# A fused attention and expert kernel: another order of the first loads, constants and attention steps, with added idle products

## The chip, the cores and the metric

The kernel runs on one core of a Trainium2 chip. The metric is the device time of one execution in microseconds; of several executions the median stands.

## The reference

Attention has two parts: a coarse one on means of four positions, and a local one in which each position sees those less than four away. Their sum, with the heads joined, is the input of a layer of eight experts, of which each row takes the one with the largest router value.

```python
q_d = q.reshape(B, H, Sd, 4, D).mean(axis=3)          # k_d, v_d likewise
out_up = np.repeat(sm_attn(q_d, k_d, v_d), 4, axis=2)
mask = np.abs(pos[:, None] - pos[None, :]) < 4
out_local = np.matmul(softmax(np.where(mask, scale * q @ k.T, -1e9)), v)
x = (out_up + out_local).transpose(0, 2, 1, 3).reshape(B * S, H * D)    # 4608 x 512
logits = x @ w_gate + modality_bias[modality_id]
e_idx = np.argmax(logits, axis=1)
for e in range(8):
    rows = e_idx == e
    out[rows] = gate_w[rows, None] * (np.maximum(x[rows] @ w1[e], 0.0) @ w2[e])
```

q, k and v are (8, 8, 576, 64) in f32; w1 is (8, 512, 1024) and w2 (8, 1024, 512).

## The kernel before, in words

Attention is cut into 32 steps n: batch n // 4, two heads in each. q and k come in halves of a batch, that is for two steps at a time (half h serves steps 2h and 2h + 1), into four pairs of buffers that take turns (called xh, xl, w and xh again in the trace); v comes by batch, in pieces of 90 KB for batch 0 and of 180 KB afterwards, into two windows (h_167, h_168). A step is a chain over all engines. PE transposes q and k (tp, L352) and their fourth rows (tpt, L365), ScalarE and DVE copy them out and sum them (qT, kT, kd L408); PE writes the band mask (mk, L417) and adds the local scores on it (sc, L426), and makes the coarse scores (scd, L449); DVE and ScalarE make the softmax (lm, le, exp, dm, de, z, zr); PE transposes the coarse weights (pdt, L513) and multiplies with v (avd L528, avl L544); DVE adds both into X (L552).

After a batch the router works on it: products with wg (lg, L612), the largest value, a count of rows for each expert, a scatter of row numbers into the table tab (L727, GpSimd), and a store of the rows to xs (L721, SyncE). For these it needs small constants: numbers 0 to 7 and a triangle of ones (`Consts.routing`), w_gate (`Consts.load`), the modalities and their biases (`Consts.biases`), and blank rows in xs and tab (`Router.start`).

Then come the experts, in units of rows. A unit's w1 is loaded raw by SyncE (L945; w2 at L947) into a ring of four buffers, and each piece is split into a high and a low part (hi by GpSimd or ScalarE at L959, lo by DVE or GpSimd at L965), since a product in this precision is made of three: hi with xh, hi with xl, lo with xh. Layer 1 of the first unit (L1136) begins while the last attention steps run: eight groups of twelve products, each group in one bank of PSUM, taken out by ScalarE (relu, L1140) and DVE (what the relu left, L1142). Layer 2 is at L1296. The units behind it use w1 in combined quarters (L1013 for the differences R, L989 and L990 for their split).

The order of the work in attention is written out by hand. Each piece of a step is a call with a key (such as `tpt:4`) and a time, which is n plus `PHASE` plus an offset from `MOVED`; all calls are sorted by that time and issued under a manual schedule, so that this order is each engine's order:

```python
def call(key, at, f, *args):
    at += MOVED.get(key, 0)
    calls.append((at, len(calls), f, args))
```

The loads of q and k (`q0` ...), v (`v00` ...), the constants (`consts`, `routing`, `start`, `biases`) and the first expert's weights and products are calls in the same list. Behind it the routing of the last batch and everything of the experts is put in order by the framework, by its own estimate of when operands are ready, after what the list issued. Idle products (L1464, eight in a group, 128x128 on zeros, into a corner of the bank Z that nobody reads) stand at two places late in the list.

The profile's names are those of the program: xh, xl and w are reused for other things; h_167 and h_168 are the two windows of v; raw is a raw weight piece.

Of the kernel before, what the change touches and what calls it, by code (L numbers as in the profile page):

```python
# [10 lines left out]
I32 = mybir.dt.int32  # L11
# [114 lines left out]
LOP = (0, 3, 4)  # L126
NL = 1
CHP = (4,)
NDA = (2, 4, 8, 10)
ZD = (1, 5, 7, 8, 9, 10)  # L130
XA = (0, 1, 2, 3)
FZ = (21, 23)
FN = 8
NZ = 24


def whole(pieces):

# [1494 lines left out]
```

## Time and profile before

| | |
|---|---|
| median of 3 executions | 652.12 us (649.57 to 653.86) |
| the profiled execution | 645.31 us, of which the span of its trace is 643.6 us |
| mean granted clock of TensorE in it | 0.988 |
| busy: PE, DVE, ACT, GpSimd (POOL) | 615.6, 488.9, 392.2, 300.8 us |

The profile comes from one execution. PE is TensorE's products, DVE is VectorE, ACT is ScalarE, POOL is GpSimd, and SP is SyncE, which issues most transfers. "Idle before" is the time an engine stood still ahead of an instruction, with what released it. The granted clock is 1.00 at 2.4 GHz and 0.50 at 1.2 GHz.

### The profile page before, as it was taken

The numbers are of one execution on the slowest core, as the hardware profiler recorded it, in microseconds if no ns is written. First come the engines' busy times: TensorE is split into PE (matmuls) and PEld (weight loads), VectorE is DVE, ScalarE is ACT, GpSimd is POOL, SyncE is SP. The second block draws the span as 40 slices with busy tenths as digits, with TensorE's granted clock in tenths as the row PEclk, the third lists the DMA queues.
The fourth block names the chain that finished last, engine by engine and source line by source line (L and its number), as shares of the span: only waits on it lengthen the run. The fifth ranks groups of instructions, "written<-read, shape, count | busy, mean of one in ns | idle before, by whom it ended". The sixth has DMA issues, their size and how long they took to land.

```text
span 643.6 us, 19370 instructions
## 1 busy us (share of the span) xinstructions
PE 615.6 (96%) x7414; PEld 516.9 (80%) x7414; DVE 488.9 (76%) x1025; ACT 392.2 (61%) x853; POOL 300.8 (47%) x356
## 2 busy tenths in 40 slices
PE   7699999999999899999999999999999999999995
PEld 4467777776766668889898898998988989989984
DVE  5667888989879858778869889788596886845450
ACT  5568878777877723466564655665665665645451
POOL 7657889889778793570410402304215023030111
PEclk9889999999999899999999999999999999999999
DMA  9799999999979866295553552635633525576821
GB/s 184 155 187 193 184 200 200 191 190 210 184 165 212 227 174 172 60 326 141 165 184 118 166 156 100 195 100 167 193 118 131 148 98 164 135 230 188 223 90 39
DMA packets 173121, 107.16 MB, mean 166 GB/s; under 512 B 132988, under 2 KB 151456, under 8 KB 173026
## 3 DMA queue, kind: packets, MB, share of 16 engines
q1 hardware_dynamic: 165810, 86.71, 56.8%
q0 software_dynamic: 7216, 19.18, 9.3%
q8 instruction: 60, 0.98, 0.7%
q14 instruction: 35, 0.29, 0.2%
HBM read 86.61 MB, written 19.51 MB: 165 GB/s over the span
## 4 chain that ended last, share of the span: by engine, by line
PE 73%; DVE 8%; DMA 6%; SPq 4%; POOL 4%; issue 3%; ACT 1%; POOLq 0%; DVEq 0%; ACTq 0%
PE l L1296 27%; PE l L1197 20%; PE l L1171 3%; DMA raw<-in_moe_w_dram 3%; PE tp L352 3%; PE scd L449 3%; PE avl L544 2%; PE sc L426 2%; PE avd L528 2%; PE xt L1088 2%; SPq L308 2%; SPq L328 1%; PE vp L340 1%; PE pdt L513 1%; PE l L1136 1%
## 5 line engine op out<-in xcount | busy, mean ns | idle before, releaser
L1307 POOL DMA_INDIRECT out_dram<-o,tg x33 | 43.7, 1326 | 165.1 <-ACT o L1299 75.9
L1296 PE MATMUL l<-whi,h 128*128 128x512 f32 (+1 forms) x356 | 109.6, 389 | 0.2 <-DVE h L1274 0.2
L1296 PEld LDWEIGHTS l<-whi,h 128*128 128x128 f32 x356 | 65.2, 188 | 13.1 <-DVE h L1274 0.5
L965 DVE TENSOR_TENSOR wlo<-raw,whi 128x1024 fp32r<-128x1024 f32 x36 | 43.7, 1230 | 33.5 <-ACT whi L959 33.0
L1296 PE MATMUL l<-wlo,h 128*128 128x512 f32 (+1 forms) x178 | 67.9, 385 | 0.0
L1197 PE MATMUL l<-xh,whi 128*128 128x256 f32 x240 | 66.3, 276 | 0.0
L1197 PE MATMUL l<-xl,whi 128*128 128x256 f32 x240 | 66.3, 276 | 0.0
L1197 PE MATMUL l<-xh,wlo 128*128 128x256 f32 x240 | 66.3, 276 | 0.0
L1296 PE MATMUL l<-whl,h 128*128 128x512 f32 (+1 forms) x240 | 57.9, 386 | 0.0
L1212 ACT ACTIVATE h<-R 128x512 fp32r<-128x512 f32 x42 | 26.4, 634 | 41.8 <-DVE R L1210 41.8
L1296 PEld LDWEIGHTS l<-whl,h 128*128 128x128 f32 x240 | 44.0, 188 | 8.6
L1057 POOL DMA_INDIRECT xg<-xs,tg x32 | 39.1, 1221 | 24.3 <-PE xt L1088 16.1
L727 POOL DMA_INDIRECT tab<-ig,si x36 | 36.5, 1014 | 21.5 <-DVE si L698 13.9
L1197 PEld LDWEIGHTS l<-xh,whi 128*128 128x128 f32 x240 | 45.1, 188 | 0.0
L1197 PEld LDWEIGHTS l<-xl,whi 128*128 128x128 f32 x240 | 45.1, 188 | 0.0
L1197 PEld LDWEIGHTS l<-xh,wlo 128*128 128x128 f32 x240 | 45.0, 188 | 0.0
L383 ACT COPY kT<-tp 64x512 f32<-64x512 f32 x64 | 37.3, 582 | 7.8 <-PE tp L352 7.1
L1197 PE MATMUL l<-xh,w 128*128 128x256 f32 x176 | 41.7, 276 | 0.0
L503 POOL TENSOR_TENSOR h<-lt,sel 128x576 f32<-128x576 f32 x32 | 36.8, 1150 | 4.8 <-DVE lt L498 2.8
L1296 PEld LDWEIGHTS l<-wlo,h 128*128 128x128 f32 x178 | 33.2, 188 | 6.7
L959 ACT CAST whi<-raw 128x1024 fp32r<-128x1024 f32 x32 | 33.1, 1049 | 8.3 <-issue 5.0
L1299 ACT ACTIVATE o<-l,tg 128x512 f32<-128x512 f32 x37 | 25.4, 686 | 20.4 <-PE l L1296 16.9
(336 smaller groups left out, 1775.1 us busy)
## 6 DMA issues: line engine op xcount, KB each, us to landing
raw<-in_moe_w_dram SPq DMA_DIRECT2D x176, 128.0 KB
raw<-in_moe_w_dram SPq DMA_DIRECT2D x44, 512.0 KB
h<-in_v_dram SPq DMA_DIRECT2D x53, 180.0 KB
xs<-R SPq DMA_DIRECT2D x64, 128.0 KB
xl<-in_k_dram SPq DMA_DIRECT2D x16, 288.0 KB
xh<-in_q_dram SPq DMA_DIRECT2D x14, 288.0 KB
xl<-in_q_dram SPq DMA_DIRECT2D x8, 288.0 KB
w<-in_k_dram SPq DMA_DIRECT2D x8, 288.0 KB
```

The source lines that it names most:

```text
L352: s.nc.tensor.transpose(p[:, 128 * j : 128 * j + 128], src[:, 5 * (n % 2) + j].rearrange("p a d -> p (a d)"), s.C.ident)
L383: s.nc.scalar.copy(s.kB[r, g, a, PAD + 64 * g : PAD + 64 * g + 512], s.t["tp", "k", n][r])
L503: s.nc.gpsimd.tensor_tensor(s.Pw[n % NPW], s.t.pop(("lt", n))[:, :, :SUB].unsqueeze(2).broadcast_to(sh), s.C.sel.unsqueeze(1).unsqueeze(3) ...
L727: i = nc.gpsimd.indirect_dma_start(out=s.tab[:, :], out_offset=bass.IndirectOffsetOnAxis(ap=C.si[:, t : t + 1], axis=0), in_=C.ig[:, t, :] ...
L959: (nc.gpsimd.tensor_copy if turn in HIP else nc.scalar.copy)(hi, raw)
L965: (nc.gpsimd if turn in LOP else nc.vector).tensor_tensor(lo, raw, hi.bitcast(F32), op=ALU.subtract)
L1057: nc.gpsimd.indirect_dma_start(out=R[:, h, :], out_offset=None, in_=s.xs[:n, :], in_offset=bass.IndirectOffsetOnAxis(ap=T[:, h, 0:1], axis ...
L1197: nc.tensor.matmul(banks[g][:, f, :], a[:, fs], b[:, x, k, :], start=start and f == k == i == 0, stop=k == 1 and i == 2, skip_group_check= ...
L1212: nc.scalar.activation(h, x, AF.Relu)
L1296: nc.tensor.matmul(p[:, cs], a[:, f, hs], x[:, f % 2, cs], start=(f == 0 and i == 0), stop=(f == 7 and i == 2), skip_group_check=last_rows)
L1299: nc.scalar.mul(o, p, T[:, h, 1:2].bitcast(F32))
L1307: nc.gpsimd.indirect_dma_start(out=s.out[:, :], out_offset=bass.IndirectOffsetOnAxis(ap=T[:, h, 0:1], axis=0), in_=o, in_offset=None, boun ...
```

## The change

Calls are cut smaller and get new times. q and k of a half are loaded by calls of their own (`k2`, `q2`, ...; half 0 in four parts, q ahead of k). `Consts.load` loses the modalities and biases to `load_bias`; the DVE part of `routing` becomes `numbers`; `Router.start` is split into `scratch` (the bank Z, first of all), `start`, and `blanks`. `warm` adds groups of `FM` = 6 idle products at five of twelve places, `y0`, `y3`, `y4`, `y8` and `y10`. About 300 keys of steps 0 to 10 get offsets in `MOVED`, or other ones. Nothing that is computed changes. Lines of the changed kernel are 48 to 59 higher (tp L406, tpt L419, sc L480, layer 1 L1195, its evictions L1199 and L1201, R L1072).

```diff
 MOVED = {
...
+    "blanks": 5.8766, ... "k2": -0.4342, "k3": -3.5596, "k4": 1.3137, ... "mi": 6.7344, "numbers": 3.5421,
+    "q2": -0.2781, "q3": -3.6701, "q4": -0.8408, ... "start": 3.1539, "tpt:4": -0.124, ... "wg": 7.5204,
...
+FY = (0, 3, 4, 8, 10)
+FM = 6
...
-    def load(s, tc, pool, work, rows, mid, bias, w_gate):
+    def load(s, tc, pool, w_gate):
...
+    def load_bias(s, tc, work, rows, mid, bias):
+        nc = tc.nc
         s.mf = rows.tile([128, 2 * DM], F32, name="R", bufs=NR)[:36, :384]
...
+    def numbers(s, tc, pool):
+        nc = tc.nc
         s.ef = pool.tile([128, NE], F32, name="ef")
-        nc.vector.tensor_copy(s.ef, ie)
+        nc.vector.tensor_copy(s.ef, s.ie)
...
-    def load_qk(s, b, half):
+    def load_qk(s, h, x, part=None):
         nc = s.nc
-        qt, kt = s.QKt[(2 * b + half) % 4]
-        for j in (slice(0, 5), slice(5, 9)) if (b, half) == (0, 0) else (slice(0, 9),):
-            for t, src in ((kt, s.k), (qt, s.q)):
-                for a in range(2):
-                    h = src[b, 4 * half + 2 * a : 4 * half + 2 * a + 2].rearrange("h s d -> (h s) d")
-                    nc.sync.dma_start(t[:, j, a], h.rearrange("(j p) d -> p j d", p=128)[:, j])
-        s.QK[2 * b + half] = (qt, kt)
+        b, half = divmod(h, 2)
+        s.QK[h] = s.QKt[h % 4]
+        src, j = (s.q, s.k)[x], slice(0, 9) if part is None else (slice(0, 5), slice(5, 9))[part]
+        for a in range(2):
+            g = src[b, 4 * half + 2 * a : 4 * half + 2 * a + 2].rearrange("h s d -> (h s) d")
+            nc.sync.dma_start(s.QK[h][x][:, j, a], g.rearrange("(j p) d -> p j d", p=128)[:, j])
...
-    def start(s, work):
-        nc, xs, tab = s.nc, s.xs, s.tab
+    def scratch(s):
         s.Z = s.ps.tile([128, 512], F32, name="Z", tag="Z", bufs=1)
+
+    def start(s):
+        nc = s.nc
         s.rev = s.Z[:, 0:NE]
...
+    def blanks(s, work):
+        nc, xs, tab = s.nc, s.xs, s.tab
         zr = work.tile([128, DM // 128], F32, name="zr")
...
-            for j in range(3):
-                call(f"q{j}", -3 + 0.1 * (j if j < 2 else 6), at.load_qk, j // 2, j % 2)
+            for j in range(4):
+                call(f"k0{j}", -3 + 0.01 * j, at.load_qk, 0, 1 - j % 2, j // 2)
+            for j in (1, 2):
+                for x, nm in ((1, "k"), (0, "q")):
+                    call(f"{nm}{j}", -3 + 0.1 * (j if j < 2 else 6) - 0.001 * x, at.load_qk, j, x)
+            call("scratch", -3.2, ro.scratch)
...
+            def warm(k):
+                if k in FY:
+                    for _ in range(FM):
+                        nc.tensor.matmul(ro.Z[:, 384:512], C.dummy, C.dummy, start=True, stop=True, skip_group_check=True)
+
+            for k in range(12):
+                call(f"y{k}", 0.7 + 0.7 * k, warm, k)
```

What the change moves on an engine is seen in the engines' orders. On SyncE, at the start of the program, from the last load of half 1 on (half 2 is xl<-in_k and xh<-in_q below the v, in_v), there stood before:

```order
L308 DMA xl<-in_q_dram 128x9x64 x2
L322 DMA h_167<-in_v_dram 27x64
L328 DMA h_167<-in_v_dram 30x11x64
L328 DMA h_167<-in_v_dram 30x12x64 x15
L308 DMA xl<-in_k_dram 128x9x64 x2
L308 DMA xh<-in_q_dram 128x9x64 x2
L206 DMA wg<-in_moe_w_gate_dram 64x2x8 x4
```

and there stand now:

```order
L363 DMA xl<-in_q_dram 128x9x64 x2
L376 DMA h_167<-in_v_dram 27x64
L382 DMA h_167<-in_v_dram 30x11x64
L382 DMA h_167<-in_v_dram 30x12x64 x7
L363 DMA xl<-in_k_dram 128x9x64 x2
L363 DMA xh<-in_q_dram 128x9x64 x2
L382 DMA h_167<-in_v_dram 30x12x64 x8
L363 DMA w_165<-in_q_dram 128x9x64 x2
L363 DMA w_166<-in_k_dram 128x9x64 x2
```

Eight pieces of v have gone behind half 2; half 3 (w_165, w_166) has come right behind them, and wg stands far below.

On PE, around the first products of half 2 (xl is its k, xh its q), where the transposes of step 4 and the scores of step 3 stand, the order before was

```order
L417 LDWEIGHTS identb
L417 MATMUL sc<-mask,identb 128x384
L352 MATMUL tp<-ident,xl 128x128 x4
L426 MATMUL sc<-kT,qT 24x64 x24
L365 MATMUL tpt<-ident,xh 128x128
L365 MATMUL tpt<-ident,xl 128x128
L449 MATMUL scd<-kd_176,h_167 64x144 x6
```

and is now

```order
L471 LDWEIGHTS identb
L471 MATMUL sc<-mask,identb 128x384
L419 MATMUL tpt<-ident,xh 128x128
L419 MATMUL tpt<-ident,xl 128x128
L480 MATMUL sc<-kT,qT 24x64 x24
L406 MATMUL tp<-ident,xl 128x128 x4
L503 MATMUL scd<-kd_176,h_167 64x144 x6
```

The two rows of tpt, which need q of half 2, have gone ahead of the scores (L426, now L480) and of the transposes of k (L352, now L406).

On DVE, where layer 1 of the first unit is taken out of PSUM (h is the eviction, l a bank of layer 1, wlo a low weight part, R the differences of the second unit's raw weights), the order before was

```order
L965 TENSOR_TENSOR wlo_5428<-raw,whi_5427 128x1024 [waits Pool_49]
L965 TENSOR_TENSOR wlo_5446<-raw,whi_5445 128x1024 [waits DMAHW1_49,Activation_49]
L1142 SCALAR_TENSOR_TENSOR h_5304<-l_5483,h_5304 128x512 [waits Activation_49]
L965 TENSOR_TENSOR wlo_5434<-raw,whi_5433 128x1024 [waits Pool_49]
L965 TENSOR_TENSOR wlo_5440<-raw,whi_5439 128x1024 [waits DMAHW4_49,Pool_49]
L742 COPY mc<-cp 128x8 [waits PE_49]
L1013 TENSOR_TENSOR R<-raw 128x512 [waits DMAHW3_49,DMAHW6_49,DMAHW2_49,DMAHW7_49,DMAHW1_49,DMAHW0_49]
L691 TENSOR_TENSOR sl<-pr,oh 128x40 [waits PE_49]
L1142 SCALAR_TENSOR_TENSOR h_5305<-l_5569,h_5305 128x512 [waits Activation_49]
L990 TENSOR_TENSOR whl<-raw,whl 128x512 [waits Activation_49]
```

with the evictions of three other groups above it, and is now (from the last wlo of this unit on)

```order
L1024 TENSOR_TENSOR wlo_5476<-raw,whi_5475 128x1024 [waits DMAHW5_49,Activation_49]
L1072 TENSOR_TENSOR R<-raw 128x512 [waits DMAHW6_49,DMAHW7_49,DMAHW1_49,DMAHW0_49]
L832 SCALAR_TENSOR_TENSOR poff<-pexcl,pbase 128x8 [waits DVE_49]
L844 TENSOR_TENSOR o<-pexcl,uf 128x48 [waits DMAHW4_49,DMAHW3_49,DMAHW2_49]
L1049 TENSOR_TENSOR whl<-raw,whl 128x512 [waits Activation_49]
L846 TENSOR_TENSOR o<-o 128x48 [waits DVE_49]
L1201 SCALAR_TENSOR_TENSOR h_5334<-l_5336,h_5334 128x512 [waits Activation_49]
L1072 TENSOR_TENSOR R<-raw,R 128x512 [waits DMAHW4_49,DMAHW5_49,DMAHW3_49,DMAHW2_49]
L850 TENSOR_TENSOR o<-o,poff 128x48 [waits DVE_49]
L1201 SCALAR_TENSOR_TENSOR h_5334<-l_5513,h_5334 128x512 [waits Activation_49]
L1072 TENSOR_TENSOR R<-raw 128x512
```

All eight evictions of layer 1 (L1142, now L1201) stand behind the first R<-raw now; before, four of them stood ahead of it. The waits in brackets name counters: DMAHW are transfers.

## Rows read from the trace of the kernel before

**Rows 1.** Page, part 1: busy time, share of the span, instructions of each engine.

```profile
PE 615.6 (96%) x7414; PEld 516.9 (80%) x7414; DVE 488.9 (76%) x1025; ACT 392.2 (61%) x853; POOL 300.8 (47%) x356
```

**Rows 2.** Windows: stretch, length, busy us of each engine, PEclk, DMA share, GB/s.

```profile
160.00:200.00 40.00, 38.51 (x918) 28.41 (x922) 33.25 (x103) 31.98 (x103) 31.57 (x41) 1.00 0.92 178
...
240.00:600.00 360.00, 359.00 (x2314) 323.88 (x2314) 281.88 (x449) 207.27 (x306) 98.34 (x84) 1.00 0.53 159
```

**Rows 3.** Windows of the start and of one later stretch.

```profile
8.00:16.00 8.00, 5.65 (x128) 4.32 (x128) 3.83 (x9) 6.02 (x15) 5.22 (x23) 1.00 1.14 195
...
27.26:37.50 10.24, 9.40 (x142) 7.32 (x145) 3.83 (x10) 5.04 (x16) 5.60 (x7) 0.50 0.83 137
...
221.80:225.30 3.50, 3.34 (x57) 2.97 (x49) 3.01 (x12) 2.04 (x8) 2.48 (x3) 0.51 0.72 263
```

**Rows 4.** Waits of PE, 0 to 50 us: total us, times, longest us.

```profile
PE sc L417 <- DVE e L237: 1.8, 1, 1.8
...
PE tpt L365 <- DMA xl<-in_q_dram: 0.8, 1, 0.8
```

**Rows 5.** Timeline of PE: start us, us, instruction xcount [idle before <-releaser].

```profile
18.12 0.87 PE L426 MATMUL sc<-kT,qT 128*24 128x64 f32 x48
...
22.87 0.34 PE L417 MATMUL sc<-mask,identb 128*128 128x384 bf16 x1
24.96 0.63 PE L352 MATMUL tp<-ident,xl 128*128 128x128 f32 x4 [1.75 <-DMA xl<-in_k_dram]
...
28.10 0.45 PE L365 MATMUL tpt<-ident,xh 128*128 128x128 f32 x1 [1.71 <-DMA xh<-in_q_dram]
...
36.09 1.50 PE L426 MATMUL sc<-kT,qT 128*24 128x64 f32 x48
...
43.80 0.66 PE L352 MATMUL tp<-ident,w 128*128 128x128 f32 x4 [1.06 <-DVE kd L408]
```

**Rows 6.** Chain of waits in order of time: start us, us, what.

```profile
22.12 5.89 DMA xh<-in_q_dram
28.10 0.66 PE tpt L365 x2
...
195.68 7.42 DMA h<-in_v_dram
203.12 5.11 DMA raw<-in_moe_w_dram
```

**Rows 7.** DMA view, 0 to 50 us: rate in 40 slices, issues with sizes.

```profile
GB/s 0 76 227 261 225 224 219 221 218 228 193 116 185 196 194 153 169 251 242 224 197 26 9 33 84 239 176 196 199 185 208 221 182 158 145 211 168 190 190 175
...
h<-in_v_dram SPq DMA_DIRECT2D x15, 90.0 KB
```

**Rows 8.** Timeline of PE around the idle products, 216 to 218 us.

```profile
216.84 0.62 PE L1464 MATMUL Z<-dummy 128*128 128x128 bf16 x8
```

**Rows 9.** Instructions of L727, 0 to 120 us: ns min/median/max, first and last start.

```profile
L727 POOL DMA_INDIRECT tab<-ig,si x10: 1010/1010/1194, 70.0 to 119.8; - x10
```

**Rows 10.** Timelines of DVE and ACT, 247 to 253 us.

```profile
247.10 0.68 DVE L1142 SCALAR_TENSOR_TENSOR h<-l,h 128x512 fp32r<-128x512 f32 x1
...
252.53 0.69 DVE L1013 TENSOR_TENSOR R<-raw 128x512 f32<-128x512 f32 x1 [2.40 <-DMA raw<-in_moe_w_dram]
...
252.51 0.62 ACT L989 CAST whl<-raw 128x512 fp32r<-128x512 f32 x1 [2.25 <-DMA raw<-in_moe_w_dram]
```

**Rows 11.** Timeline of GpSimd, 233 to 239 us.

```profile
233.49 2.40 POOL L965 TENSOR_TENSOR w<-raw,w 128x1024 fp32r<-128x1024 f32 x1
...
238.84 3.02 POOL L959 CAST whi<-raw 128x1024 fp32r<-128x1024 f32 x3
```

**Rows 12.** Timeline of PE in layer 1 and at layer 2's start.

```profile
244.64 0.39 PE L1136 MATMUL l<-xh,whi 128*128 128x512 f32 x1
...
246.91 0.39 PE L1136 MATMUL l<-xh,whi 128*128 128x512 f32 x1
...
255.85 0.61 PE L1296 MATMUL l<-whi,h 128*128 128x512 f32 x2
```

More of the change, by code (lines that the diff above doesn't have):

```diff
@@ L212, in load, with routing @@
         nc.sync.dma_start(s.bb, bias.unsqueeze(0).broadcast_to([128, 2, NE]))
-    def routing(s, tc, pool, work, psum):
+    def routing(s, tc, pool, work):
         nc = tc.nc
@@ L225, in routing @@
         s.si = pool.tile([128, 36], I32, name="si")
-        ie = work.tile([128, NE], I32, name="ie")
-        nc.gpsimd.iota(ie, pattern=[[1, NE]], base=0, channel_multiplier=0)
+        s.ie = work.tile([128, NE], I32, name="ie")
+        nc.gpsimd.iota(s.ie, pattern=[[1, NE]], base=0, channel_multiplier=0)
+        s.iu = work.tile([128, NUMAX], I32, name="iu")
+        nc.gpsimd.iota(s.iu, pattern=[[1, NUMAX]], base=0, channel_multiplier=0)
+    def numbers(s, tc, pool):
+        nc = tc.nc
         s.ef = pool.tile([128, NE], F32, name="ef")
-        nc.vector.tensor_copy(s.ef, ie)
+        nc.vector.tensor_copy(s.ef, s.ie)
         s.rev = pool.tile([128, NE], F32, name="rev")
@@ L238, in routing @@
         s.e2 = s.e2.rearrange("p t e -> p (t e)")
-        iu = work.tile([128, NUMAX], I32, name="iu")
-        nc.gpsimd.iota(iu, pattern=[[1, NUMAX]], base=0, channel_multiplier=0)
         s.uf = pool.tile([128, NUMAX], F32, name="uf")
-        nc.vector.tensor_copy(s.uf, iu)
+        nc.vector.tensor_copy(s.uf, s.iu)
         n = 2 * NE
@@ L1356, in call @@
                 calls.append((at, len(calls), f, args))
-            for j in range(3):
-                call(f"q{j}", -3 + 0.1 * (j if j < 2 else 6), at.load_qk, j // 2, j % 2)
+            for j in range(4):
[4 more added lines that the diff above has]
+            call("scratch", -3.2, ro.scratch)
             for j in range(4):
                 call(f"v0{j}", -2.8 + 0.1 * j, at.load_v, 0, 2 * j, 2)
-            call("consts", -2.3, C.load, tc, cp, work, at.wk, mid, bias, w_gate)
+            call("wg", -2.3, C.load, tc, cp, w_gate)
+            call("mi", -2.299, C.load_bias, tc, work, at.wk, mid, bias)
             P = PHASE
@@ L1382, in build @@
             for h in range(3, N // 2):
-                call(f"q{h}", 2 * h - 4.4, at.load_qk, h // 2, h % 2)
+                for x, nm in ((1, "k"), (0, "q")):
+                    call(f"{nm}{h}", 2 * h - 4.4 - 0.001 * x, at.load_qk, h, x)
             for j in range(3):
@@ L1388, in build @@
             call("sums", 0.95, C.sums, nc)
-            call("routing", 2.05, C.routing, tc, cp, work, ps)
-            call("start", 2.55, ro.start, work)
+            call("routing", 2.05, C.routing, tc, cp, work)
+            call("numbers", 2.051, C.numbers, tc, cp)
+            call("start", 2.55, ro.start)
+            call("blanks", 2.551, ro.blanks, work)
             call("biases", 5.05, C.biases, tc, cp, work, at.wk, ps)
```

146 rows, old and new, of the table MOVED are left out of this document.

## The prediction, made before the changed kernel had run

> **What bounds the kernel now.** I read four views, from the whole to the place. The page's busy times first: TensorE (PE) is busy 615.6 us of a 643.6 us span, and no other engine passes 489 us [rows 1]. So time can only come from PE's gaps, from products that run slowly, or from work that is added to PE. The windows view then says where the gaps are. From 240 to 600 us PE is busy 359.00 of 360 us, and from 160 to 200 us 38.51 of 40 [rows 2]; at the start it is busy only 5.65 of the 8 us from 8 to 16 [rows 3], and the granted clock falls soon after. The windows put the half clock (0.50, so 1.2 GHz) on 27.26 to 37.50 us, with PE busy for 9.40 us of it [rows 3]. The list of PE's waits in the first 50 us and PE's timeline name the gaps, 0.8 to 1.8 us each, and show what follows them [rows 4, 5]. The chain of waits says what the last of them hangs on: one transfer, xh<-in_q, from 22.12 to 28.01 us [rows 6]. That is q of half 2 (steps 4 and 5), and it is issued behind sixteen pieces of v.
>
> **The start, part by part.** All sums are made against the profiled execution, 645.31 us; the median of the timed runs is 652.12 us, 6.8 us more, and I carry differences over to it.
>
> The loads of half 2. Eight pieces of v, 90 KB each [rows 7], now go behind q and k of half 2. They are 720 KB; the DMA rate in those slices is 185 to 228 GB/s [rows 7], so q comes 3.2 to 3.9 us earlier. I take 3.7, so it lands at 24.3 us and not at 28.0. PE finishes the mask product in front of it at about 23.2 us, as before [rows 5]. Before, it then waits 1.75 us, does the transposes (0.57 us to the next start) and the scores of step 3 (0.87 us), and waits 1.71 us [rows 5]. In the new order the transposes of q and k together (tpt) come first of these, so PE waits 1.1 us, and the other two follow while nothing is missing: tpt (0.66 us [rows 6]) is done at 25.0, the rest at 26.4 against 28.8 us. Gain 2.4 us; the ends are 0 and 3.7 us (no wait at all in front).
>
> The clock. From 27.26 to 37.50 us PE is busy 9.40 us at 0.50 [rows 3]. The 48 products of sc take 1.50 us there and 0.87 us at full clock [rows 5]: a ratio of 0.58, so some 4.0 us of the 9.40 are lost to the clock. Before the fall PE had two waits of 1.7 to 1.8 us within 5 us. The new order leaves one of 1.1 us there; by the sums above PE is busy more of that stretch than of the one from 8 to 16 us, where 5.65 of 8 us went by with the clock at 1.00 [rows 3]. I take the whole 4.0 us; the other end is 0.
>
> The row says 4.0 us for 10.24 us at 0.50 [rows 3]. The Trainium skill (TensorE: Matmul & The Clock Gate, Terms) puts the penalty at the throttled time times the share of pulses withheld; that is 10.24 x 0.5 = 5.1 us, an estimate by that page, and the sum at the end would be +0.3 by it. The trace doesn't agree in full, since some of the time in that stretch didn't stretch with the clock, and the measured ratio decides.
>
> The numbers of the routing. Their DVE block (ef to ltri) stands behind the first steps now; PE's 1.8 us wait for e [rows 4] goes. GpSimd's block for the sums still stands ahead of the first products with q, so what comes next there is late too: I take 0.7 us, with ends 0 and 1.8.
>
> The idle products. Five groups of six. Eight of them take 0.62 us at full clock [rows 8], so 0.47 us for six. The first group lies in a wait; the other four stand where PE has work: +1.9, and with a little for the joints +2.0 us; ends 0 and 2.4 (five groups).
>
> Biases, wg, the blanks of xs and tab. The biases' DVE work holds PE's transposes for 1.06 us [rows 5]; it now comes later, in a stretch where DVE is as full, so the wait moves: 0, ends -1.1 and +1.1. The filling of tab is moved behind half 5's loads. The first scatter into tab starts at 70.0 us [rows 9], some 5 us earlier in the changed kernel; the loads that went ahead of it are about 3.7 MB, 19 us at that rate, on a landing at 45 us. It should land a little ahead of that scatter, and its cover is thin: 0, at worst +1. Half 0's q ahead of k changes which of two transposes waits first: 0, within 0.8 [rows 4].
>
> The start: -2.4 - 4.0 - 0.7 + 2.0 = -5.1 us. It keeps until the experts' work begins if nothing else paces the middle: DVE 33.25 and GpSimd 31.57 of 40 us from 160 to 200 us, PE 38.51 [rows 2], so PE still sets the pace. From 194 to 213 us the chain runs through transfers (h<-in_v 7.42 us, then two of raw<-in_moe_w, the first 5.11 us [rows 6]), but these are issued when buffers come free, so they move with PE.
>
> **Where the first expert layer begins.** The same table shifts what the framework orders by itself around 229 to 290 us, and there the rows are the other way round. Before, the evictions of the first four layer-1 groups stand ahead of the wait on DVE for the second unit's raw weights; that wait lasts 2.40 us, ends at 252.53 us, and costs PE nothing [rows 10]. In the changed order all evictions stand behind it on DVE, and on ScalarE behind a cast of the same raw weights. The low part of the fourth weight piece (GpSimd, w lo), done before at 235.9 us, now stands behind the clearing of xg and three casts, which end at 241.9 us before [rows 11] and later once they wait for the last stores to xs, so the first groups can't end before about 247 us either.
>
> PE needs the first free bank at its sixth group. Its first five groups are 60 products; before, the 49th starts at 244.64 and the 59th at 246.91 us [rows 12], 0.227 us apart, so the 60th is done at 247.4, and with the routing products that now stand there at 247.6 us. The bank comes free after this: raw weights landed 252.5 (as before [rows 10]); DVE makes the first R (0.69 [rows 10]), subtracts whl over as many columns, and after some 0.2 us of small work evicts (0.68 [rows 10]): 254.7 us. PE waits 7.1 us. The two corrections nearly cancel: DVE comes to the first wlo up to 1.8 us earlier, as three evictions no longer stand ahead of it, and the 512 KB load of the last weight piece now stands right ahead of these loads, not 10 us ahead: up to +2.5. I take 6.5 us. The low end is 0.7 us, one eviction, if the weights are there already; the high end 9.6. The remaining 36 products then run behind one another as before, and PE has no gap left between 240 and 600 us in which to take it back: 1.0 us in all [rows 2].
>
> The sum: -5.1 + 6.5 = +1.4, that is 646.7 us in a profiled execution like this one, and 652.12 + 1.4 = **653.5 us** on the median.
>
> **The rivals.**
>
> The late order costs little: the weights land before PE needs the bank, or DVE gets through earlier. For it speaks that the wait on DVE before cost PE nothing. Against it, 252.5 us is a landing that was measured, not one that is argued. Then only the start counts: 652.12 - 5.1 + 0.7 = 647.7 us; I give it 3 us to both sides, since the timed runs may hold more of the half clock than the profiled one.
>
> The slower side: the clock gate. The wait of 6.5 us at 248 us is longer than those that went ahead of the fall at 27.26, and at the start the clock may fall in spite of the new order, since several waits of about 1 us remain. Price 4.0 us each, by the stretch at half clock [rows 3]. With the late fall alone 657.5 us; with both 661.5 us. It decides the sign outright: with even one of them the change is slower than before. For it: the kernel before has a second stretch near half clock, 221.8 to 225.3 us at 0.51 [rows 3], behind a stretch with short waits. Against: layer 1 is unbroken work on either side of the wait. The Trainium skill (TensorE: Matmul & The Clock Gate, Part 1, on what is actually happening) calls the throttled state the default, which activity releases; by that rule a wait alone brings the clock down, and no run of this case shows one like this inside layer 1.
>
> The change doesn't do what it says: k of half 4 now stands behind a batch of v and the biases, and if it lands after about 49 us the wait at the start merely moves from half 2 to half 4. Then the start gives 2 us and not 5.1, and the time is 656.6 us with the late wait.
>
> More comes at the start than the rows show (a longer half clock in the timed runs) and the late order costs little: 642 us.
>
> **How the numbers follow.** Forecast, both terms as worked out: 0.42, its own range 649.5 to 657. The late order free: 0.30. The clock gate: 0.13. Half 4 late: 0.08. More at the start: 0.07. A measurement of this kernel can tell about 1%, 6.5 us, from no change. Faster by more than that (below 645.6) needs the last case and half of the second, with some of the timed spread: 0.26. Slower (over 658.6) needs most of the clock's case and the tail of half 4 and of the forecast: 0.18. The rest, 0.56, lies within. The range from 643 to 661 leaves out the far part of the two outer cases.
>
> **What would show it.** In the changed kernel's trace: xh<-in_q of half 2 lands at 24.3 us and PE's first tpt of it starts there; the granted clock stays 1.00 from 24 to 40 us; the transposes of step 6, at 43.80 us before [rows 5], start near 38; the fifth layer-1 group, at 244.64 us before [rows 12], near 239.5. Then PE's list of waits shows one of 5 to 8 us in the layer-1 line, ended by a DVE eviction, and layer 2, at 255.85 us before [rows 12], starts later than 255. The prediction is wrong at the start if the clock is still at 0.50 anywhere before 40 us, and wrong at the late term if PE has no wait over 2 us between 240 and 260 us.

## The result, and the profile after

The changed kernel takes 660.06 us (658.58 to 661.54, 6 runs), the kernel before 651.28 us (648.62 to 653.86, 6 runs) beside it: a ratio of 1.0141, with an interval of 1.0118 to 1.0163. So it is 8.8 us slower: inside the range given (643 to 661), near its end, outside the forecast's own range (649.5 to 657), and 6.6 us from the point (653.5). The profiled execution takes 658.58 us, with a span of 656.6 us.

The page's first lines, as in [rows 1]:

```profile
span 656.6 us, 19430 instructions
...
PE 619.8 (94%) x7444; PEld 520.4 (79%) x7444; DVE 489.6 (75%) x1025; ACT 392.2 (60%) x853; POOL 298.9 (46%) x356
```

PE is busy 4.2 us longer, of which the thirty idle products are 2.5, and the span is 13.0 us longer than in the first profile of the kernel before. The windows, as in [rows 2, 3] (stretch, length, busy us of PE, PEld, DVE, ACT, GpSimd, clock, DMA):

```profile
8.00:16.00 8.00, 4.85 (x64) 3.89 (x64) 1.77 (x7) 4.11 (x9) 3.97 (x17) 0.67 1.24 206
10.67:17.50 6.83, 5.53 (x109) 4.68 (x109) 1.81 (x3) 3.20 (x7) 3.43 (x12) 0.50 1.18 201
160.00:200.00 40.00, 37.22 (x807) 26.86 (x809) 31.30 (x94) 28.63 (x89) 30.12 (x37) 0.96 0.90 178
240.00:600.00 360.00, 350.31 (x2263) 315.12 (x2262) 272.91 (x439) 199.86 (x297) 98.66 (x86) 0.99 0.52 155
253.02:263.26 10.24, 4.20 (x10) 3.33 (x11) 6.71 (x14) 4.82 (x8) 3.31 (x4) 0.50 0.54 105
```

From 240 to 600 us PE now stands still 9.7 us where it stood still 1.0 us, and there is a stretch at half clock, 253.02 to 263.26 us, in the middle of layer 1. From 160 to 200 us PE is busy 1.3 us less than before. At the start the half clock hasn't gone: it lies at 10.67 to 17.50 us and not at 27.26 to 37.50, so that the window from 8 to 16 us, at 1.00 before, stands at 0.67. The wait of 1.8 us that [rows 4] puts down to e is gone, and the list of waits has others (the waits of PE in the first 50 us, total us, times, longest):

```profile
PE sc L480 <- ACT kT L437: 2.5, 1, 2.5
...
PE tp L406 <- ACT qT L426: 1.0, 1, 1.0
PE tpt L419 <- DMA xh<-in_k_dram: 0.9, 1, 0.9
...
PE sc L471 <- DVE le L489: 0.4, 1, 0.4
```

The same view for 240 to 600 us has one long row, for the sixth group of layer 1:

```profile
PE l L1195 <- DVE h L1201: 9.2, 1, 9.2
```

PE's timeline in the start, as in [rows 5] (tpt of half 2, tp of its k, tp of step 6):

```profile
24.66 0.27 PE L419 MATMUL tpt<-ident,xh 128*128 128x128 f32 x1
...
25.77 0.66 PE L406 MATMUL tp<-ident,xl 128*128 128x128 f32 x4
...
37.16 0.66 PE L406 MATMUL tp<-ident,w 128*128 128x128 f32 x4
```

and from the first product of layer 1 to layer 2, as in [rows 12] (the row of 245.71 is the first product of the fifth group, that of 248.42 holds the last products of the first five):

```profile
231.58 0.51 PE L1195 MATMUL l<-xh,whi 128*128 128x512 f32 x1 [0.27 <-ACT xh L1176]
...
245.71 0.39 PE L1195 MATMUL l<-xh,whi 128*128 128x512 f32 x1
...
248.42 1.41 PE L1195 MATMUL l<-xh,w 128*128 128x512 f32 x5
259.06 0.79 PE L1195 MATMUL l<-xh,whi 128*128 128x512 f32 x1 [9.23 <-DVE h L1201]
...
263.63 0.40 PE L1195 MATMUL l<-xh,w 128*128 128x512 f32 x1
...
270.23 0.62 PE L1355 MATMUL l<-whi,h 128*128 128x512 f32 x2
```

The first products with q of half 2 start at 24.66 us (28.10 before), those with its k at 25.77 (24.96), step 6 at 37.16 us (43.80 before); the first layer-1 product starts at 231.58 us (229.61 before), the fifth group at 245.71 (244.64 before), layer 2 at 270.23 (255.85 before). What stands around PE's wait of 9.23 us is seen on the other engines, as in [rows 10, 11]. DVE:

```profile
245.61 2.36 DVE L1024 TENSOR_TENSOR wlo<-raw,whi 128x1024 fp32r<-128x1024 f32 x2
...
253.75 1.26 DVE L1024 TENSOR_TENSOR wlo<-raw,whi 128x1024 fp32r<-128x1024 f32 x1 [2.21 <-issue]
256.79 0.69 DVE L1072 TENSOR_TENSOR R<-raw 128x512 f32<-128x512 f32 x1 [1.78 <-DMA raw<-in_moe_w_dram]
...
258.32 0.69 DVE L1201 SCALAR_TENSOR_TENSOR h<-l,h 128x512 fp32r<-128x512 f32 x1
```

ScalarE:

```profile
252.67 1.04 ACT L1018 CAST whi<-raw 128x1024 fp32r<-128x1024 f32 x1 [8.06 <-issue]
256.78 0.62 ACT L1048 CAST whl<-raw 128x512 fp32r<-128x512 f32 x1 [3.06 <-DMA raw<-in_moe_w_dram]
```

GpSimd, as in [rows 11]:

```profile
238.46 3.01 POOL L1018 CAST whi<-raw 128x1024 fp32r<-128x1024 f32 x3
241.44 2.38 POOL L1024 TENSOR_TENSOR w<-raw,w 128x1024 fp32r<-128x1024 f32 x1
```

The weight loads that SyncE issues (start and length of the issuing, xcount issues):

```profile
246.86 0.40 SPq L1006 DMA_DIRECT2D raw<-in_moe_w_dram  x1
248.00 6.16 SPq L1004 DMA_DIRECT2D raw<-in_moe_w_dram  x8
```

The chain reads like this. DVE's two wlo run from 245.61 to 247.97 us and free a raw buffer each. The first goes to the 512 KB load (issued at 246.86), so the raw weights of the second unit are issued from 248.00 on. ScalarE and DVE have only a cast and a wlo left to do (252.67, 253.75) and then wait: ScalarE's cast of the new weights starts at 256.78 and DVE's first R at 256.79, both released by that transfer. The first eviction is DVE's at 258.32, and PE starts its sixth group when it ends, at 259.06, though its own last product had ended at 249.83. GpSimd's low part ends at 243.82 and holds nobody. The same loads before:

```profile
246.07 3.96 SPq L945 DMA_DIRECT2D raw<-in_moe_w_dram  x8
```

They were the first that SyncE issued there, 6.46 us ahead of the first R at 252.53 [rows 10]; now it is 8.79 us.

### The profile page after: what moved, and what is told of

It reads as the page before. It is cut to its first block, busy times and chain, and to the rows that moved or that the text cites. A ratio compares the mean times of both kernels' runs of the same rounds, so it can differ in the third digit from the quotient of the medians.

```text
span 656.6 us, 19430 instructions
## 1 busy us (share of the span) xinstructions
PE 619.8 (94%) x7444; PEld 520.4 (79%) x7444; DVE 489.6 (75%) x1025; ACT 392.2 (60%) x853; POOL 298.9 (46%) x356
## 4 chain that ended last, share of the span: by engine, by line
PE 82%; DVE 7%; issue 3%; POOL 3%; ACT 2%; DMA 1%; SPq 0%; POOLq 0%; DVEq 0%; ACTq 0%
PE l L1355 30%; PE l L1256 20%; PE tp L406 4%; PE sc L480 3%; PE l L1230 3%; PE avl L598 3%; PE scd L503 3%; PE l L1195 3%; PE avd L582 2%; PE xt L1147 2%; PE vp L394 2%; PE pdt L567 2%; DMA raw<-in_moe_w_dram 1%; PE sc L471 1%; PE lg L671 1%
## 5 line engine op out<-in xcount | busy, mean ns | idle before, releaser
L1116 POOL DMA_INDIRECT xg<-xs,tg x32 | 36.8, 1151 | 40.1 <-PE xt L1147 18.1
```

What stands on the lines that cost most here:

```text
L1116: nc.gpsimd.indirect_dma_start(out=R[:, h, :], out_offset=None, in_=s.xs[:n, :], in_offset=bass.IndirectOffsetOnAxis(ap=T[:, h, 0:1], axis ...
```

## The experiments

All ratios are against the kernel before in runs on the same chip. Two findings on the program's order stand behind these experiments. What the framework orders by itself, from about step 28 on, hangs on the number of instructions in the first steps: leaving out six idle products of thirty puts everything there back into exactly the order of the kernel before, and a few idle products in the kernel before bring exactly the order of the changed one.

**The late order, taken away and put in.**

e1, the changed kernel without the group y3:

```diff
-FY = (0, 3, 4, 8, 10)
+FY = (0, 4, 8, 10)
```

> The changed kernel without its second group of idle products (y3, six of thirty); with that, the framework puts everything behind step 28 in exactly the order of the kernel before. Theory (the late order is the loss, the start a gain of about 3 us): 648 us (646 to 650), no PE wait over 2 us in layer 1, no half clock at 250 us. Rival (the start or the idle products themselves cost the time): 658 to 660 us as the changed kernel, whatever the late order.

Measured: 650.17 us, ratio 1.0007 (0.9985 to 1.0029). PE has no wait over 0.3 us in layer 1, and no half clock there. Six idle products fewer take away the whole loss; but the start's gain of some 5 us isn't there either.

e2, none of them:

```diff
-FY = (0, 3, 4, 8, 10)
+FY = ()
```

> The changed kernel without any of its idle products, late order again that of the kernel before. If idle products only cost their own time where PE has work (four groups of 0.47 us, 24 left in e1): 1 to 2 us under e1, 646 to 647 us. If they hold the clock up at the start, as a rival has it: a longer half clock in the first 40 us and a time over e1's, 650 us or more.

Measured: 649.38 us, ratio 0.9984 (0.9965 to 1.0004), 0.8 us under e1. In this execution the clock stays at 1.00 in the whole start, without any idle product:

```profile
0.00:40.00 40.00, 32.07 (x604) 22.14 (x606) 25.23 (x66) 25.20 (x71) 26.80 (x64) 1.00 0.98 192
```

So the start's clock can stay up without the idle products. One execution says little here, though, since the half clock moves from one execution to the next (below): e8, which has no idle product either, is at 0.50 from 10.86 to 17.69 us.

e3, the kernel before with the changed kernel's function `warm` and two groups of eight; e4 has the same with `FM = 10`:

```diff
+FY = (3, 4)
+FM = 8
```

> The kernel before with two groups of eight idle products in steps 2 to 4, which leave its start as it was, but with which the framework gives everything behind step 28 exactly the order that it has in the changed kernel. Theory (late order costs about 12 us): 661 to 665 us, a PE wait of 7 to 10 us in layer 1 and half clock behind it. Rival (the late order costs little, the changed start is the loss): 652 to 654 us.

> The same as e3 with ten and not eight idle products in each of the two groups; the framework's late order is then that of the kernel before but for nine rows. Theory: 652 to 654 us (1 us of idle products), so that e3 less e4 is the late order alone, 9 to 12 us. Rival (idle products in the first steps are what costs): 660 us or more.

Measured: e3 660.82 us, ratio 1.0150 (1.0108 to 1.0193); e4 651.16 us, ratio 1.0020 (1.0001 to 1.0039). e4 has four idle products more than e3 and is 9.7 us faster. The start is the old one in both. So the late order alone is worth 9.7 us, with some 3 us to either side, about what the whole change costs. The two traces agree on where: from the first product of layer 1 to layer 2 it is 36.67 us in e3 and 26.46 in e4, 10.2 us more, and behind that 0.7 us less. (The first product itself comes 2.3 us later in e3, whose start was at half clock for 10.24 us in this execution and for 3.4 us in e4's.) PE's longest wait from 235 to 285 us in e3 (lines are 2 higher than in the kernel before):

```profile
PE l L1138 <- DVE h L1144: 7.5, 1, 7.5
```

and in e4:

```profile
PE l L1138 <- ACT xh L1119: 0.3, 1, 0.3
```

e3 also has a stretch at half clock behind its wait, 259.58 to 266.41 us; e4 has none there.

e9, twelve products more put into the wait (the fifth group's, made twice):

```diff
+                    if (g, k, f) == (2, 3, 5):
+                        for j in range(1):
+                            for z in range(4):
+                                (wh, wl), (xh, xl) = W[z], X[0]
+                                for i, (a, x) in enumerate(((wh, xh), (wh, xl), (wl, xh))):
+                                    nc.tensor.matmul(p[f], a[:, 128 * f : 128 * f + 128], x[:, z, :], start=(z == 0 and i == 0),
+                                                     stop=(z == 3 and i == 2))
```

> The changed kernel with the twelve products of the fifth layer-1 group done twice (the same values into the same bank), right ahead of the sixth group: 2.7 us of PE work more, in the place of the wait. Theory (PE waits there for DVE and ScalarE, which wait for the raw weights, so the sixth group starts when it starts): 659 to 661 us as the changed kernel, the wait at the sixth group 6.5 us and not 9.2. Rival (PE's own products set when the sixth group can start, or the evictions follow PE): 662.5 to 663.5 us.

Measured: 657.58 us, ratio 1.0174 (1.0131 to 1.0218), which overlaps that of the changed kernel and can't by itself tell 0 from 2.7 us; on this chip, where the kernel before takes 646.4 us, the theory asks for 655.5 us and the rival for 658.2, and the middle lies nearer the rival. The trace tells them apart: PE's wait at the sixth group is shorter by just the 2.7 us that were put in.

```profile
PE l L1195 <- DVE h L1208: 6.5, 1, 6.5
```

The sixth group starts 27.4 us behind the first product of layer 1, and 27.5 us in the changed kernel. PE isn't what sets that time; DVE's eviction, behind the weights, is.

**The start.**

e5, the kernel before once more, with no edit:

> The kernel before once more, for a second profile of it: the first one (645.3 us) lies under all its timed executions, and it alone of the six profiles so far has no idle pieces of 0.4 to 0.5 us on PE between 192 and 212 us that end with an instruction's issue. Theory (the first profile is not typical): span 648 to 651 us, those idle pieces are there, first layer-1 product near 233 us and not 229.6. Rival (they come with the changed kernels alone): 644 us and none of them.

Measured: 649.03 us, span 647.2. The first layer-1 product starts at 233.63 us, and idle pieces put down to the issue of instructions are there. PE's waits, 190 to 215 us:

```profile
PE sc L426 <- issue: 1.9, 4, 0.5
PE avl L544 <- issue: 1.1, 3, 0.5
```

and four of them in the timeline:

```profile
203.18 0.25 PE L426 MATMUL sc<-kT,qT 128*24 128x64 f32 x2 [0.43 <-issue]
203.92 0.24 PE L426 MATMUL sc<-kT,qT 128*24 128x64 f32 x2 [0.49 <-issue]
204.66 0.30 PE L426 MATMUL sc<-kT,qT 128*24 128x64 f32 x4 [0.49 <-issue]
205.42 0.22 PE L426 MATMUL sc<-kT,qT 128*24 128x64 f32 x1 [0.47 <-issue]
```

In the first 50 us the wait of 1.8 us that [rows 4] puts down to e is put down to ScalarE here (two waits, the longer is this one):

```profile
PE sc L417 <- ACT de L462: 2.2, 2, 1.8
```

There is another difference, which the theory didn't name. In the start this execution was at half clock for 3.4 us only, and not for 10.24:

```profile
26.40:29.80 3.40, 3.40 (x62) 2.57 (x62) 0.85 (x2) 1.67 (x4) 2.23 (x2) 0.50 0.16 22
```

Its step 8 begins at 52.10 us and its step 12 at 76.96, against 55.16 and 79.41 in the first profile. The changed kernel's stand at 51.34 and 76.19: a lead of 0.8 us over this profile, where the first one made it 3.2 to 3.8.

e6, the kernel before with k and q of half 2 ahead of eight pieces of v, and nothing else:

```diff
-    "pr:6": 0.4434, "q15": -1.6, "qT0:29": -0.0983, "qT1:26": -0.1157, "qT1:28": -0.4423, "qT1:30": -0.0375,
+    "pr:6": 0.4434, "q2": -0.25, "q15": -1.6, "qT0:29": -0.0983, "qT1:26": -0.1157, "qT1:28": -0.4423, "qT1:30": -0.0375,
```

> The kernel before with one offset more: k and q of half 2 are loaded behind eight pieces of v and not sixteen; nothing else of the first steps is moved. The prediction's first two terms alone. By them q lands at 24.3 us and not 28.0, PE runs tpt 3.7 us earlier, and the half clock of 27 to 37 us goes: 4 to 7 us under before, 643 to 646 us. Rival (whatever is won at the start is lost again before the experts begin): 649 to 651 us, with step 12 earlier by 3 us and the first layer-1 product no earlier.

Measured: 651.20 us, ratio 1.0016 (0.9994 to 1.0038). q lands at 24.20 us as worked out, and step 4 begins at 24.36 us (26.05 in e5). PE is 3.3 us ahead of e5 when it comes to half 3, and there it waits:

```profile
36.09 0.32 PE L417 MATMUL sc<-mask,identb 128*128 128x384 bf16 x1 [0.34 <-ACT de L462]
39.84 1.09 PE L352 MATMUL tp<-ident,w 128*128 128x128 f32 x4 [3.43 <-DMA w<-in_k_dram]
```

The clock falls with that wait (it also stood at 0.50 for 3.4 us before, from 17.46 us on):

```profile
37.92:44.76 6.84, 4.92 (x68) 3.69 (x70) 2.69 (x9) 2.77 (x7) 3.40 (x4) 0.50 1.00 187
```

Step 12 begins at 77.77 us, later than in e5 (76.96). So the start's lead does go, and not slowly before the experts: it is gone within two steps, because the next load is then the late one and the clock falls in the wait for it.

e7 and e8 ask whether transfers eat a lead later on. In both, v of batches 2 to 7 isn't loaded, so that those batches are computed with older v; other numbers of rows then go to the experts, and the times are to be compared with each other alone.

```diff
-                if b + 1 < B:
+                if b < 1:
```

> The kernel before, in which v of batches 2 to 7 is not loaded, so that the windows keep older data: about 8.6 MB less of transfers before 200 us, the same instructions on the other engines. Theory (transfers pace the stretch from 150 to 215 us): the first layer-1 product comes 3 us or more earlier than in e5. Rival (PE's own work paces it): within 1 us.

> The changed kernel without idle products (e2), and without the loads of v of batches 2 to 7, as in e7. With all transfers e2 is 0.8 us under before though its step 12 comes 4.2 us earlier. Theory (transfers eat the lead between 150 and 215 us): here the lead stays, e8 is 3 to 5 us under e7, in time and at the first layer-1 product. Rival (the lead is lost to something else, PE's instruction issue or another engine): e8 within 1.5 us of e7, as e2 is of before.

Measured: e7 689.87 us (ratio 1.0592, 1.0545 to 1.0639), e8 687.31 us (1.0562, 1.0521 to 1.0603). The first layer-1 product starts at 233.88 us in e7 (233.63 in e5), though the DMA engines are busy only 0.61 of the time from 80 to 120 us, where they are at 0.98 in the first profile of the kernel before:

```profile
80.00:120.00 40.00, 38.71 (x949) 28.90 (x942) 35.84 (x108) 31.49 (x102) 35.48 (x46) 1.00 0.61 128
```

So transfers don't pace the middle, and the theory's 3 us fall. (Between step 12 and layer 1 PE was at half clock for 6.8 us in e7 and for 3.4 in e5, which can hide 1.7 us at most.) e8 leads e7 by 1.2 us at step 12 and by 1.1 us at the first layer-1 product; in time it is 2.6 us under e7, between what theory and rival asked for, with intervals that overlap. The lead of the new start isn't eaten on the way; it is small from the beginning.

**Other late orders, and the best start.**

e10 and e11 have six evictions ahead of the first R where the kernel before has four. e10 is the changed kernel with the one group below; e11 is e3 with `FM = 6`; e12 is the changed kernel with `FY = (0,)`, the group that lies in a wait, and has the late order of the kernel before.

```diff
-FY = (0, 3, 4, 8, 10)
+FY = (3,)
```

> The changed kernel with one of its five groups of idle products (y3) alone. With it the framework puts six of the eight layer-1 evictions ahead of the first R and not four as before. Theory (what counts is that PE never waits for a bank in layer 1; four ahead were enough): 649 to 650 us, as e2 within its interval. Rival (more evictions ahead win more): 646 to 648 us, faster than before and than e2.

> The kernel before with two groups of six idle products in steps 2 to 4, its start else as it was, and with the late order of e10 (six evictions ahead). Against e4 (twenty idle products, four evictions ahead, 651.2 us). Theory: 650 to 651 us, the difference of eight idle products. Rival: 647 to 648.5 us.

> The changed kernel with the first of its five groups of idle products alone (y0, which lies in a wait of PE); late order that of the kernel before. e2, with none, came to 0.9984 of before (0.9965 to 1.0004). Theory (the first group costs nothing and the new start is worth a few tenths of a per cent): ratio 0.996 to 0.999, step 12 near 75 us. Rival (the new start is worth nothing): 1.000 to 1.002. By the prediction's own start term without the costly groups (7 us): 0.989.

Measured: e10 650.81 us, ratio 1.0055 (1.0024 to 1.0086); e11 650.98 us, 1.0055 (1.0027 to 1.0082); e12 645.59 us, 1.0018 (0.9988 to 1.0048), on chips on which the kernel before took 646.43 and 643.73 us. More evictions ahead win nothing; both are slower than before by some 3.6 us. Their traces show a new wait in the second unit's layer 1, for GpSimd's split of the raw weights, of 2.2 us in e10 and 2.5 us in e11; e1, e2, e4, e5 and e12 have none over 1 us there. PE's waits, 235 to 340 us, in e10:

```profile
PE l L1256 <- POOL whl L1049: 2.2, 1, 2.2
```

and the stretch right behind it, at half clock, where PE is busy throughout, so that it loses about half of it:

```profile
282.80:286.20 3.40, 3.40 (x18) 3.40 (x17) 2.64 (x3) 0.70 (x2) 3.09 (x2) 0.50 1.04 389
```

2.2 us and 1.7 us make 3.9 us, of 3.6 measured, with 2.0 us to either side. From layer 2's start to the end of the span it is 392.2 us in e10 and 392.5 in e11, and 387.3 to 388.7 in those five. Why GpSimd is late there wasn't tested. The new start, with its free idle group, isn't faster than the old one. No version here beats the kernel before by more than the runs can tell; e2, at 1.0 us, comes nearest.

## Why the prediction was right, and where it was wrong

The sign was forecast (+1.4), the size not (+8.8). The forecast's own range ended at 657 us; the time lies in the wide range only because that had room for the rivals. Both terms were off, the first by more.

"The start: -2.4 - 4.0 - 0.7 + 2.0 = -5.1 us." It measured nothing that can be told from zero with four of the five idle groups (e1, +0.5 us with 1.4 us to either side), with the free one alone (e12, +1.2 with 1.9 to either side), and -1.0 us without any (e2). By its steps:

- The loads of half 2. The landing was right (24.3 forecast; tpt starts at 24.66). Step 6 "near 38" came true too (37.16), but its place in PE's order is another one, and step 8 is only 0.8 us ahead of e5. What failed is that the gain would stand. e6 does this step alone and wins nothing: PE arrives earlier at half 3, whose load it then waits for 3.4 us. The rival that had the wait move named half 4; it was the half before it. The changed kernel moves half 3 forward too, but it also puts q of half 0 ahead of k, and the first scores then wait 2.5 us for kT: the step that the prediction priced at "0, within 0.8" (no run undoes it alone).
- The clock, 4.0 us, was the largest term and the weakest. It was taken from one execution with 10.24 us at half clock. The second profile of the same kernel has 3.4 us there, by the same ratio (0.42 of it) 1.4 us. And it wasn't removed: the half clock now lies at the new wait of 2.5 us, which ends at 11.97 us. Of the seven profiles with the new start six are at 0.50 for 3.4 or 6.8 us from 10.67 to 13.12 us on (6.8 us in the changed kernel, 3.4 in e1), and only e2 isn't. That the clock stays at 1.00 from 24 to 40 us came true, and "anywhere before 40 us", the mark of a wrong prediction, did too.
- The numbers of the routing, 0.7 us, rested on a wait that the first profile puts down to DVE's e. ScalarE's de ends at 17.39 us there and e at 17.42. In all six other profiles with the old start the same wait of 1.8 us is put down to de, as in e5. So the numbers held PE up there for 0.03 us at most. In the changed order that wait is gone, and the one of 2.5 us above stands in its place.
- The idle products, 2.0 us for thirty: e1 less e2 is 0.8 us for 24 of them, e4 less before 1.3 us for 20. Both have over 1 us to either side, so the term is not refuted, and its size not shown.
- "They move with PE", of the late loads: e7 and e8 agree, within 1.7 us, that transfers don't hold the middle up.

With the start's gain went the place of the fifth layer-1 group, forecast near 239.5 us and found at 245.71.

"I take 6.5 us", the late order. The mechanism was right in each link: the evictions behind R, R behind the raw weights, the sixth group behind the first eviction, ended by DVE. It measured 9.7 us (e3 less e4), at the given high end of 9.6. In the trace of the changed kernel layer 2 starts 38.65 us behind the first product of layer 1, before (229.61 to 255.85) 26.24 us: 12.4 us more. Of these, 9.2 are the wait, where the working had 7.1 ahead of its corrections. PE was ready 18.25 us behind the first product (18.0 by the working, 247.6 - 229.6), and the raw weights were there 25.2 us behind it (22.9, 252.5 - 229.6): the difference is the landing. Both corrections happened, and they didn't cancel. DVE did come to its first wlo earlier, by 1.2 us (14.0 us behind the first product, 244.83 - 229.61 = 15.2 before), but the buffer that this freed went to the last piece's 512 KB load; the raw weights were issued 16.4 us behind the first product in both kernels, and then took 2.3 us longer to come (8.79 for 6.46). That the load ahead of them makes all of this was not tested by itself: with the same order it is 8.77 us in e9 but 7.26 in e3, and 5.2 to 6.7 in e1, e2, e4, e5, e6 and e12, which have the order of before. In e3 the wait is 7.5 us. So the two corrections together came to +2.1 us in the changed kernel and to +0.4 in e3, where the prediction took -0.6. The GpSimd part, which was to hold the first groups until "about 247 us", ended at 243.8.

Another 2.1 us are the clock, and this was a rival: behind the wait the sixth group's twelve products take 4.8 us, from 259.06 to 263.86, for 2.7 us at full clock (12 by the 0.227 us of the working). It had a chance of 0.13 and a price of 4.0 us; with a fall at the start as well it gave 661.5 us, of all the cases named the one nearest to the time. It came in all three profiles with the wait: the changed kernel, e3 (7.5 us) and e9 (6.5 us). The price was half of the one given, because PE stood still for most of the 10.24 us. The waits of 2.2 us (e10), 2.5 us (e11) and 3.4 us (e6) have a stretch at 0.50 at their end too; e1, e2, e4, e5 and e12 have no wait over 1 us from 235 to 330 us, and a clock of 1.00 there. The Trainium skill (TensorE: Matmul & The Clock Gate, Part 1, on what is actually happening) calls the throttled state the default, which activity releases; the granted clocks behind these six waits agree. Against, "layer 1 is unbroken work on either side of the wait" was no protection. The last 1.1 us of the 12.4 are other work that now stands between, 0.8 of it the eight products xt at 263.86. Some of this comes back: from layer 2's start to the end of the span it is 386.4 us now and was 387.8. In e3 against e4 the same parts are 7.5 us of wait, 1.9 of clock and 0.8 of xt.

So the forecast had one term too large by about 5 us and one too small by 3; the late fall of the clock, which it had left to a rival, is 2 of these 3. That the sum still had the right sign is owed to the late term alone.

The rival that "the late order costs little" fell with e1 and e3; its ground, that DVE's wait had cost PE nothing before, held only because four evictions stood ahead of it.

## What to carry to other kernels

Where part of an order is made by a scheduler from estimates, a few instructions added early can turn a far place over: compare the whole order, engine by engine, and look there for work that frees a buffer standing behind a wait for a transfer. That kind of loss was worth 9.7 us here and could be read before any run; with a ring of buffers, count also who takes the first one that comes free. A gain in the first steps needs the load behind the next one too, and a clock term needs more than one profile.

## What the runs showed of the hardware that was not expected

One profile isn't the kernel. Between 190 and 215 us PE stands still in pieces of 0.4 to 0.5 us, one each few products, that the trace puts down to the issue of instructions: 3.3 us in the second profile of the kernel before, 2.8 to 3.8 us in the changed kernel, e1, e2, e3, e4 and e6, and none in the first profile of the kernel before. They go with the chip as far as is known: 2.8 to 3.8 us on the two chips on which the kernel before takes 650.2 and 649.7 us, 0.6 to 1.5 us, in one or two pieces (e9, e10, e11), where it takes 646.4, and 0.2 us (e12) where it takes 643.7. The first profile's chip isn't on record, so it may have been taken on a faster one than the timed runs. They stay with fewer transfers (e7, e8). They are as long as 3.3 of the 6.8 us by which the first profile (645.3 us) lay under the median of its timed runs; what makes PE's instructions late there wasn't settled.

The half clock of the start moves between profiles of one kernel: 27.26 to 37.50 us in the first, 26.4 to 29.8 us in the second. And a wait of only 2.2 us, between long stretches of unbroken products, had a fall behind it (e10). The length of the longest wait alone doesn't decide it: behind the wait of 2.5 us in its start e2 had none, and the changed kernel stands at 0.50 from 194.99 to 198.40 us with no wait over 0.9 us in the 20 us ahead.
